# Transposed q and k for the later batch pairs: small block loads and a VectorE transpose in place of TensorE transposes

## The chip, the core and the metric

The kernel runs on one core of a Trainium2 chip. The metric is the device time of one execution in microseconds. The profile is of one execution of the same kernel; its span runs from the first to the last instruction.

## What is computed

The program is a retention block (attention without softmax, with a decay mask) followed by a multiplicative feed-forward block, all in float32; the four weights arrive as float64 and are converted on the chip.

```python
# q, k, v: (8 batches, 8 heads, 576 positions, 64)
scores = (1/8) * q @ k^T ;  D[n,m] = gamma_h ** (n-m) for n >= m, else 0
x = ((scores * D) @ v)            # then (B,H,S,64) -> (4608 tokens, 512)
a = x @ w1 ; b = x @ w2           # 512 -> 1024
out = ((a * b) @ w3) @ w_out      # 1024 -> 1024 -> 512
```

The decay is split into two factors, `decay_q[h, n] = gamma^n / 8` on q and `decay_k[m, h] = gamma^-m` on v, so that only a triangular 0/1 mask is left for the diagonal blocks.

## The kernel before

**Tiling.** The eight batches are taken as four pairs, the 576 positions as five chunks: one short chunk of 64 rows and four of 128. A group `g` is one chunk of one pair, so there are 20 groups; `NC` is 5, and groups 5 to 19 are the "later pairs" that the change touches. For a group, `load` (L106) brings k, q and v, each as a tile of positions by 16 heads by 64, 512 KB for a full chunk. `scale` multiplies q and v by their decays on GpSimd (L171). `front` (L185) transposes k and q on TensorE, sixteen transposes for a group (two tensors, two batches, four head pairs), and ScalarE copies the results out of PSUM into `kT` and `qT` (L188). `state` (L221) adds k^T v to a running state, `score` (L200) multiplies kT by qT, VectorE applies the mask (L203), and `pv` (L249 for the state's part, L256 for the chunk's own part) makes x. `state` is left out for the last chunk of a pair, and the L249 part for the first. The k that `state` reads is the one in natural layout, q is needed only transposed.

**The feed-forward.** `up` (L451) makes a and b for one block of 384 tokens and one block of 256 weight columns, by seven Strassen-like products; VectorE adds them up (L456) and multiplies a by b (L477). `w3_mm` (L406) folds w3 and w_out into one matrix once. `down` (L557) multiplies a*b by that matrix, again in seven products, with VectorE sums around it (L523, L527, L529, L561), and its rows are stored by `store` (L602). `strassen_tokens` (L425) makes sums of x on GpSimd for `up`.

**Order.** The order of instructions on each engine is written out by hand, and every engine takes its own in that order. After the weights' part comes the loop over groups 5 to 19 (L757). An iteration `g` holds: loads of q and k for `g+2`; `scale` of v and `front` for `g+1`; the first half of the iteration's feed-forward items (`work`); `pv(g)`; the load of v for `g+2`; `state(g+1)` and `score(g+1)`; `scale` of q for `g+2`; the second half of the items. The list of items grows as x becomes available: the iterations of groups 5 to 9 have one item each, the later ones two to four.

**Queues and buffers.** Nearly all DMAs are issued from the SP engine's queue, in program order: loads of q, k, v, the weights and the stores of the result. An SP instruction that waits (for a buffer to come free, or for a result to store) holds all that are behind it. The tiles `ld_k`, `ld_q`, `ld_v` have two buffers each; after the first pair, `kT` has one and `qT` two. GpSimd's order around the loop is `scale` of v for `g+1`, `scale` of q for `g+2`, with `strassen_tokens` between them where an item needs it.

Of the kernel before, what the change touches and what calls it, by code (L numbers as in the profile page):

```python
# [8 lines left out]
F32 = mybir.dt.float32  # L9
I32 = mybir.dt.int32  # L10
U32 = mybir.dt.uint32
ALU = mybir.AluOpType
PSUM = bass.MemoryType.PSUM

# [19 lines left out]
def kernel(  # L36
# [13 lines left out]
    nc = tc.nc  # L50
    moe_w1, moe_w2, moe_w3, moe_w_out = (
        w.bitcast(I32).rearrange("r (c t) -> r c t", t=2) for w in (moe_w1, moe_w2, moe_w3, moe_w_out))
    B, H, S, D = q.shape
# [3 lines left out]
    P = 128  # L57
    NP = H // 2
# [3 lines left out]
    NC = (S + P - 1) // P  # L62
    short = S - (NC - 1) * P
    sizes = [short] + [P] * (NC - 1)
    starts = [0] + [short + c * P for c in range(NC - 1)]
    G = NB2 * NC
# [9 lines left out]
    const = ctx.enter_context(tc.tile_pool(name="const", bufs=1))  # L76
# [8 lines left out]
    pools = {}  # L85

    def open_attention(part):
        for nm in ("ld", "fr"):
            pools[nm] = part.enter_context(
                tc.tile_pool(name=nm, bufs=2, side="right", reuse_waits="tile"))  # L90

    open_attention(att_part)
    acc = ctx.enter_context(tc.tile_pool(name="acc", bufs=7, space=PSUM))
    st_ps = ctx.enter_context(tc.tile_pool(name="st_ps", bufs=1, space=PSUM))

    ctx.enter_context(tc.manual_schedule())

    live = {}

    def load(g, names, engine=nc.sync):  # L100
        i, c = divmod(g, NC)
        sz = sizes[c]
        src = {"k": k, "q": q, "v": v}
        for nm in names:
            t = pools["ld"].tile([P, 2 * H, D], F32, tag="ld_" + nm, name="ld_" + nm)
            engine.dma_start(  # L106
                t[:sz], src[nm][2 * i:2 * i + 2, :, starts[c]:starts[c] + sz, :].rearrange("b h p d -> p (b h) d"))
            live[nm, g] = t
# [13 lines left out]
    nc.vector.memset(lim[:, 1:2], 255.0 * 2.0 ** 23)  # L122
    gk = const.tile([P, NC, H], F32, tag="gk", name="gk")
    gq = const.tile([P, NC, H], F32, tag="gq", name="gq")
    dq = ffn.tile([P, 4, 2, TB], F32, tag="c", name="dq", bufs=1).rearrange("p a b s -> p (a b s)")[:H, :S]
    nc.scalar.dma_start(dq, decay_q)
    nc.scalar.dma_start(gk[:short, 0, :], decay_k[:short, :])
# [4 lines left out]
    for c in (0, slice(1, NC)):  # L132
        n = short if c == 0 else P
# [16 lines left out]
    def strassen_weights(fp):  # L150
# [8 lines left out]
        live["S", fp] = True  # L159
        yield  # L160

    def scale(g, nm, scalar=False):
        c = g % NC
        sz = sizes[c]
        t, gam = live[nm, g], {"q": gq, "v": gk}[nm]
        t = t[:sz].rearrange("p (b h) d -> p b h d", b=2)
        if scalar:
            for h in range(H):
                nc.scalar.mul(t[:, :, h, :], t[:, :, h, :], gam[:sz, c, h:h + 1])
            return  # L170
        nc.gpsimd.tensor_tensor(  # L171
            out=t, in0=t, in1=gam[:sz, c].unsqueeze(1).unsqueeze(3).to_broadcast([sz, 2, H, D]), op=ALU.mult)

    def front(g, names="kq"):
        c = g % NC
        sz = sizes[c]
        for nm in names:
            src = live[nm, g]
            dst = pools["fr"].tile([P, 2, NP, P], F32, tag=nm + "T", name=nm + "T",
                                   bufs=1 if nm == "k" and g >= NC else 2)  # L180
            for b in range(2):
                tp = acc.tile([P, NP, P], F32, tag="acc", name="tp")
                for p in range(NP):
                    h = b * H + 2 * p
                    nc.tensor.transpose(tp[:, p, :sz],  # L185
                                        src[:sz, h:h + 2, :].rearrange("p a d -> p (a d)"),
                                        ident[:sz, :sz])
                nc.scalar.copy(dst[:, b, :, :sz], tp[:, :, :sz])  # L188
            live[nm + "T", g] = dst
# [17 lines left out]
    def state(g):  # L207
        c = g % NC
        sz = sizes[c]
        if c == NC - 1:  # L210
            return
        kn, vs = live["k", g], live["v", g]
        if c == 0:
            live["st"] = st_ps.tile([P, 2, NP, D], F32, tag="st", name="st")
        st = live["st"]

        for b in range(2):
            for p in range(NP):
                for j, hs in enumerate(heads):
                    h = b * H + 2 * p + j  # L220
                    nc.tensor.matmul(st[hs, b, p, :], kn[:sz, h, :], vs[:sz, h, :],  # L221
                                     start=(c == 0 and b == 0 and p == 0), stop=(c == NC - 2),
                                     skip_group_check=True)
        sb = pools["fr"].tile([P, 2, NP, D], F32, tag="sb", name="sb")
        nc.scalar.copy(sb, st)
        live["sb", g + 1] = sb

    def pv(g):
        i, c = divmod(g, NC)
        sz = sizes[c]  # L230
        live["x", g] = True
        qT, vs, pm = live["qT", g], live["v", g], live["pm", g]

        parts = []
        for n in range(NB):
            lo, hi = max(starts[c], n * TB), min(starts[c] + sz, (n + 1) * TB)
            if lo < hi:
                m = i * NB + n
                if ("xT", m) not in live:
                    live["xT", m] = xps[m % 4 == 3].tile([P, NP, 2, TB], F32, tag="xT", name="xT")  # L240
                parts.append((live["xT", m], lo - n * TB, lo - starts[c], hi - lo))

        banks = [acc.tile([P, 2, 2, P], F32, tag="acc", name="xps") for r in range(2)]
        order = [(b, n) for b in range(2) for n in range(2)]
        if c > 0:
            for m, (b, n) in enumerate(order):
                for r, j in ((0, 0), (0, 1), (1, 0), (1, 1)):
                    p = 2 * r + n
                    nc.tensor.matmul(banks[r][heads[j ^ r], b, n, :sz], live["sb", g][heads[j], b, p, :],  # L249
                                     qT[heads[j], b, p, :sz], start=(m == 0), stop=False,  # L250
                                     skip_group_check=True)
        for m, (b, n) in enumerate(order):
            for r in range(2):
                for half in range(2):
                    p, j = 2 * r + n, half ^ r
                    nc.tensor.matmul(banks[r][heads[half], b, n, :sz], vs[:sz, b * H + 2 * p + j, :],  # L256
                                     pm[:sz, b, j, p, :sz], start=(c == 0 and m == 0), stop=True,
                                     skip_group_check=True)
        for x, to, fr, n in parts:
            for r in range(2):  # L260
                nc.scalar.copy(  # L261
                    x[:, 2 * r:2 * r + 2, :, to:to + n].rearrange("p n b s -> p b n s"),
                    banks[r][:, :, :, fr:fr + n])
# [272 lines left out]
    def ahead(x, y, n=3):  # L536
        todo_sums = pair_of(x, y)[2]
        for _ in range(min(n, len(todo_sums))):
            aside.append(todo_sums.pop(0))
# [132 lines left out]
    att_part.close()  # L672


    pools["ab3"] = weights_part.enter_context(tc.tile_pool(name="ab3", bufs=1, side="right", reuse_waits="tile"))
    pools["wst"] = w3_part.enter_context(tc.tile_pool(name="wst", bufs=2, side="right", reuse_waits="tile"))
    w3op = ctx.enter_context(tc.tile_pool(name="w3op", bufs=1, reuse_waits="tile"))
# [34 lines left out]
    carry(2, 2)  # L712
    weights_part.close()
    open_attention(ctx)
    for g in (NC, NC + 1):
        load(g, "kqv")
    keep_stores.clear()
    store()
    todo = [(down, (0, 0), (0, 1)), (down, (1, 0), (1, 1)), (down, (0, 2), (1, 2))]
# [18 lines left out]
    def work(n):  # L738
        for _ in range(min(n, len(todo))):
            fn, *args = todo.pop(0)  # L740

            nxt = next((x for x in todo if x[0] is not carry), None)
            if nxt and nxt[0] is down and fn is not carry:
                if fn is down:
                    args.append(nxt[1:])
                else:
                    last = args == [*every[max(nxt[1][0], nxt[2][0])], NQ - 1]
                    ahead(*nxt[1:], 1 if last else 3)
            fn(*args)

    scale(NC, "q")
    scale(NC, "v")
    front(NC)
    state(NC)
    score(NC)
    scale(NC + 1, "q")
    for g in range(NC, G):  # L757
        c = g % NC
        n = -(-len(todo) // (NC - c))
        if g + 2 < G:  # L760
            load(g + 2, "kq")
        if g + 1 < G:
            scale(g + 1, "v")
            front(g + 1)
        work((n + 1) // 2)
        pv(g)
        if g + 2 < G:
            load(g + 2, "v")
        if g + 1 < G:
            state(g + 1)  # L770
            score(g + 1)
        if g + 2 < G:
            scale(g + 2, "q")
        if g == NC + 1:
            strassen_tokens(1, 0)
            todo.extend((up, 1, 0, fp) for fp in range(2))
        work(n // 2)
        if c == NC - 1:
            add_pair(g // NC)
# [44 lines left out]
```

## Time and profile before

The times are those of three runs, the rest is from the page of the profile and from the trace.

| What | Value |
|---|---|
| time, median (lowest to highest) | 888.04 us (887.27 to 888.92) |
| profiled span | 885.9 us |
| transposes of k and of q (L185), 160 each | 21.1 and 20.7 us busy |
| copies of kT and qT out of PSUM on ScalarE (L188), 40 each | 19.9 and 20.3 us busy |
| scaling of q on GpSimd (L171), 18 instructions | 34.8 us busy, 1.93 us each |
| loads of k and q, 512 KB each | 6.5 and 7.1 us from issue to landing |
| packets of all DMAs | 125,555, of which 113,704 under 512 bytes |

Busy times on different engines overlap and can't be added. "Idle before" counts only for an engine that sets the end. Matmul durations overlap one another: sixteen transposes whose mean is 0.27 us follow each other in 1.75 to 1.90 us. The chain that ended last, in order of time, shows how long such a batch holds TensorE.

### The profile page before, as it was taken

What the parts mean: (1) busy time and instruction counts of PE and PEld (TensorE: products, weight loads), DVE (VectorE), ACT (ScalarE), POOL (GpSimd) and SP (SyncE); (2) the same over time, 40 slices, a digit from 0 to 9 for tenths busy, and PEclk for the clock granted to TensorE, in tenths of its full rate; (3) what the DMA queues carried; (4) which work ended last, traced back from release to release, by engine and by line L of the source; (5) the groups of instructions that cost most, each with busy time, mean ns of one, the idle gap of its engine ahead of it and who ended that gap; (6) DMA issues with size and microseconds to landing.
All of it is one profiled execution on the core that took longest, in us unless ns stands there. A gap on an engine that the chain in (4) does not pass through costs nothing.

```text
span 885.9 us, 15255 instructions
## 1 busy us (share of the span) xinstructions
PE 866.6 (98%) x6517; PEld 792.8 (89%) x6517; DVE 433.7 (49%) x763; ACT 212.4 (24%) x426; POOL 111.1 (13%) x82
## 2 busy tenths in 40 slices
PE   5899999999999999999999999999999999999998
PEld 4799999544889999999999999999999999999997
DVE  3799998971543243433434433433433424434343
ACT  3676334552122212111121111211110111001000
POOL 3000020003003223002112121221200101000000
PEclk9999999999999999999999999999999999999999
DMA  9993332427046533134033134022100000000001
GB/s 184 217 229 99 96 118 97 143 95 107 0 108 124 105 60 73 26 72 96 1 72 61 25 72 95 1 57 40 26 24 24 1 24 1 24 24 1 24 1 47
DMA packets 125555, 59.73 MB, mean 67 GB/s; under 512 B 113704, under 2 KB 113704, under 8 KB 125488
## 3 DMA queue, kind: packets, MB, share of 16 engines
q1 hardware_dynamic: 123824, 58.47, 29.9%
q8 instruction: 51, 0.84, 0.4%
q10 hardware_dynamic: 1664, 0.30, 0.2%
q14 instruction: 16, 0.13, 0.1%
HBM read 49.32 MB, written 9.44 MB: 66 GB/s over the span
## 4 chain that ended last, share of the span: by engine, by line
PE 89%; DVE 3%; issue 1%; DMA 1%; ACT 1%; ACTq 0%; SPq 0%; DVEq 0%
PE up L451 45%; PE po L557 24%; PE ps L406 6%; PE xps L256 4%; PE sc L200 3%; PE tp L185 3%; PE xps L249 2%; PE st L221 1%; DVE c L456 1%; PE tp L396 1%; DVE e L341 0%; DMA raw<-in_moe_w_dram 0%; ACT e L330 0%; DVE w L350 0%; DVE ab L477 0%
## 5 line engine op out<-in xcount | busy, mean ns | idle before, releaser
L456 DVE TENSOR_TENSOR c<-up,c 128x384 f32<-128x384 f32 x240 | 133.6, 557 | 224.3 <-PE up L451 218.0
L451 PE MATMUL up<-xT,wA 128*128 128x192 f32 x1152 | 212.6, 328 | 0.9 <-ACT xT L261 0.9
L451 PEld LDWEIGHTS up<-xT,wA 128*128 128x128 f32 x1152 | 191.0, 191 | 3.2 <-ACT xT L261 1.1
L451 PE MATMUL up<-T,wS 128*128 128x192 f32 x768 | 141.7, 328 | 2.1 <-DVE T L425 2.1
L451 PEld LDWEIGHTS up<-T,wS 128*128 128x128 f32 x768 | 128.3, 191 | 2.4 <-issue 2.4
L557 PE MATMUL po<-w3o,ab 128*128 128x256 f32 x456 | 104.1, 380 | 0.3 <-ACT ot L579 0.3
L557 PEld LDWEIGHTS po<-w3o,ab 128*128 128x128 f32 x456 | 85.9, 190 | 12.2 <-ACT ot L579 0.7
L471 ACT COPY c<-up 128x384 f32<-128x384 f32 x48 | 22.9, 477 | 228.1 <-PE up L451 223.9
L561 DVE TENSOR_TENSOR ot<-po,ot 128x256 f32<-128x256 f32 x90 | 38.2, 424 | 74.8 <-PE po L557 74.2
L451 PE MATMUL up<-xT,wS 128*128 128x192 f32 x384 | 70.6, 327 | 0.6 <-DVE c L456 0.5
L451 PE MATMUL up<-T,wA 128*128 128x192 f32 x384 | 70.3, 326 | 0.0
L203 DVE TENSOR_TENSOR pm<-sc,mask 128x512 f32<-128x512 f32 (+1 forms) x80 | 45.5, 629 | 48.0 <-PE sc L200 48.0
L557 PE MATMUL po<-wB,forms 128*128 128x256 f32 x288 | 65.1, 379 | 0.0
L451 PEld LDWEIGHTS up<-xT,wS 128*128 128x128 f32 x384 | 63.6, 190 | 1.5 <-DVE c L456 1.5
L451 PEld LDWEIGHTS up<-T,wA 128*128 128x128 f32 x384 | 63.7, 190 | 0.0
L557 PEld LDWEIGHTS po<-wB,forms 128*128 128x128 f32 x288 | 54.7, 190 | 7.4
L171 POOL TENSOR_TENSOR ld_q<-ld_q,gq 128x1024 f32<-128x1024 f32 (+1 forms) x18 | 34.8, 1931 | 209.7 <-DMA ld_q<-in_q_dram 204.4
L406 PE MATMUL ps<-wo,w3T 128*128 128x512 f32 x128 | 56.4, 593 | 0.2 <-ACT w3T L398 0.2
L171 POOL TENSOR_TENSOR ld_v<-ld_v,gk 128x1024 f32<-128x1024 f32 (+1 forms) x17 | 32.3, 1900 | 176.5 <-DMA ld_v<-in_v_dram 144.1
L425 POOL TENSOR_TENSOR T<-xT,T 128x384 f32<-128x384 f32 x20 | 21.2, 1058 | 228.9 <-PE up L451 227.2
L477 DVE TENSOR_TENSOR ab<-c 128x768 f32<-128x768 f32 x48 | 46.4, 967 | 3.8
L406 PEld LDWEIGHTS ps<-wo,w3T 128*128 128x128 f32 x128 | 23.7, 190 | 27.3 <-issue 26.8
(72 smaller groups left out, 829.1 us busy)
## 6 DMA issues: line engine op xcount, KB each, us to landing
raw<-in_moe_w_dram SPq DMA_DIRECT2D x24, 512.0 KB, 3.8
ld_k<-in_k_dram SPq DMA_DIRECT2D x16, 512.0 KB, 6.5
ld_q<-in_q_dram SPq DMA_DIRECT2D x16, 512.0 KB, 7.1
ld_v<-in_v_dram SPq DMA_DIRECT2D x16, 512.0 KB, 4.7
out_dram<-ot SPq DMA_DIRECT2D x24, 256.0 KB, 2.1
raw<-in_moe_w_dram SPq DMA_DIRECT2D x16, 256.0 KB, 6.4
raw<-in_moe_w_out_dram SPq DMA_DIRECT2D x8, 512.0 KB, 3.5
out_dram<-ot SPq DMA_DIRECT2D x24, 128.0 KB, 2.4
```

Source lines behind the costliest of these rows:

```text
L171: nc.gpsimd.tensor_tensor(out=t, in0=t, in1=gam[:sz, c].unsqueeze(1).unsqueeze(3).to_broadcast([sz, 2, H, D]), op=ALU.mult)
L185: nc.tensor.transpose(tp[:, p, :sz], src[:sz, h:h + 2, :].rearrange("p a d -> p (a d)"), ident[:sz, :sz])
L200: nc.tensor.matmul(sc[j][:sz, p, :sz], kT[hs, b, p, :sz], qT[hs, b, p, :sz], start=True, stop=True)
L203: nc.vector.tensor_mul(pm[:sz, b, j, :, :sz], sc[j][:sz, :, :sz], mask[:sz, :sz].unsqueeze(1).to_broadcast([sz, NP, sz]))
L256: nc.tensor.matmul(banks[r][heads[half], b, n, :sz], vs[:sz, b * H + 2 * p + j, :], pm[:sz, b, j, p, :sz], start=(c == 0 and m == 0), stop ...
L406: nc.tensor.matmul(ps, live["w3T", ft][:, g, :], live["wo"][:, g, :], start=(g == 0), stop=(g == KF - 1))
L451: nc.tensor.matmul(ps[:, w, :], a[:, w, r, :], b[:, r, :], start=(new and w == r == 0), stop=(w == r == 1), skip_group_check=True)
L456: nc.vector.tensor_add(c[:, to], ps, c[:, sb])
L471: nc.scalar.copy(c[:, 0], p1)
L477: nc.vector.tensor_mul(ab[:, 4 * fp:4 * fp + 4, :], c[:, :, 0, :], c[:, :, 1, :])
L557: nc.tensor.matmul(ps[nm], a[A][:, f, :], live["W"][B][:, f, :], start=(f == 0 and not on), stop=(f == NP - 1), skip_group_check=True)
L561: nc.vector.tensor_add(ot[:, to[0], to[1]], ps[nm], ot[:, sb[0], sb[1]])
```

## The change

For groups 5 to 19, q and k are no longer transposed by TensorE. A transpose of 64-wide heads in pairs is a transpose of 128x128 made of a 4 by 4 grid of 32x32 blocks. `load_blocks` lets the DMA put each 32x32 block where it belongs after the transpose, and VectorE transposes within the blocks, one instruction for a whole tensor of a group. Its parts:

- `load_blocks` issues sixteen DMAs for each tensor of a full chunk, eight for a short one. Each fills 32 partitions with eight head pairs by 32 elements, so that a contiguous run is 128 bytes and a DMA holds 32 KB.
- The tiles `bl_k` and `bl_q` have one buffer each, so the loads for the next group wait until VectorE has read the present ones. They are placed right after `front_blocks`.
- `scale_blocks` applies the q decay on GpSimd in the new layout, in two instructions, with factors `gqs` that are loaded once by sixteen small DMAs of single 4-byte elements, at about 100 us.
- `front_blocks` is two VectorE transposes, after the first half of `work` instead of `front` ahead of it.
- k is also still loaded in natural layout for `state`, but not for a pair's last chunk.
- The first pair's groups stay as they were.

```diff
+    gqs = const.tile([P, NP, S // 32], F32, tag="gqs", name="gqs")
...
+    BL = 32
+
+    def load_blocks(g, nm):
+
+        i, c = divmod(g, NC)
+        n = sizes[c] // BL
+        t = pools["ld"].tile([P, 2 * NP, P // BL, BL], F32, tag="bl_" + nm, name="bl_" + nm, bufs=1)
+        src = {"k": k, "q": q}[nm][2 * i:2 * i + 2].rearrange("b (p a) s d -> a (b p) s d", a=2)
+        for a in range(2):
+            for f in range(D // BL):
+                part = (a * (D // BL) + f) * BL
+                for m in range(n):
+                    s0 = starts[c] + m * BL
+                    nc.sync.dma_start(t[part:part + BL, :, m, :],
+                                      src[a, :, s0:s0 + BL, f * BL:(f + 1) * BL].rearrange("m r x -> r m x"))
+        live["bl_" + nm, g] = t
+
+    def scale_blocks(g):
...
+        for b in range(2):
+            part = t[:, b * NP:(b + 1) * NP, :n, :]
+            nc.gpsimd.tensor_tensor(
+                out=part, in0=part, in1=gqs[:, :, n0:n0 + n].unsqueeze(3).to_broadcast([P, NP, n, BL]),
+                op=ALU.mult)
+
+    def front_blocks(g):
...
+        for nm in "kq":
+            dst = pools["fr"].tile([P, 2, NP, P], F32, tag=nm + "T", name=nm + "T", bufs=1 if nm == "k" else 2)
+            nc.vector.transpose(
+                dst[:, :, :, :sizes[c]].rearrange("p b m (n x) -> p (b m) n x", x=BL),
+                live["bl_" + nm, g][:, :, :n, :])
...
+    for a in range(2):
+        for f in range(D // BL):
+            part = (a * (D // BL) + f) * BL
+            for p in range(NP):
+                nc.sync.dma_start(gqs[part:part + BL, p, :], decay_q[2 * p + a].rearrange("(n r) -> r n", r=BL))
...
-    for g in (NC, NC + 1):
-        load(g, "kqv")
+    load(NC, "kv")
+    load_blocks(NC, "k")
+    load_blocks(NC, "q")
+    load(NC + 1, "kv")
...
-    scale(NC, "q")
+    scale_blocks(NC)
     scale(NC, "v")
-    front(NC)
+    front_blocks(NC)
+    load_blocks(NC + 1, "k")
+    load_blocks(NC + 1, "q")
     state(NC)
     score(NC)
-    scale(NC + 1, "q")
+    scale_blocks(NC + 1)
     for g in range(NC, G):
...
-        if g + 2 < G:
-            load(g + 2, "kq")
+        if g + 2 < G and (g + 2) % NC != NC - 1:
+            load(g + 2, "k")
         if g + 1 < G:
             scale(g + 1, "v")
-            front(g + 1)
         work((n + 1) // 2)
+        if g + 1 < G:
+            front_blocks(g + 1)
+        if g + 2 < G:
+            load_blocks(g + 2, "k")
+            load_blocks(g + 2, "q")
         pv(g)
...
         if g + 2 < G:
-            scale(g + 2, "q")
+            scale_blocks(g + 2)
```

More of the change, by code (lines that the diff above doesn't have):

```diff
@@ L160, in strassen_weights @@
         yield
+    BL = 32
[13 more added lines that the diff above has]
+    def scale_blocks(g):
+        c = g % NC
+        n, n0 = sizes[c] // BL, starts[c] // BL
+        t = live["bl_q", g]
+        for b in range(2):
[4 more added lines that the diff above has]
+    def front_blocks(g):
+        c = g % NC
+        n = sizes[c] // BL
+        for nm in "kq":
[3 more added lines that the diff above has]
+                live["bl_" + nm, g][:, :, :n, :])
+            live[nm + "T", g] = dst
     def scale(g, nm, scalar=False):
@@ L179, in front @@
             dst = pools["fr"].tile([P, 2, NP, P], F32, tag=nm + "T", name=nm + "T",
-                                   bufs=1 if nm == "k" and g >= NC else 2)
+                                   bufs=2)
             for b in range(2):
@@ L211, in state @@
             return
-        kn, vs = live["k", g], live["v", g]
+        vs = live["v", g]
+        kn = live["k", g]
         if c == 0:
```

## The prediction

> **What bounds the kernel now.** I read the page's busy times, then the chain of waits that ended last, then its pieces in order of time around the groups that change, then the SP queue's own timeline. The first two:
>
> ```profile
> PE 866.6 (98%) x6517; PEld 792.8 (89%) x6517; DVE 433.7 (49%) x763; ACT 212.4 (24%) x426; POOL 111.1 (13%) x82
> ...
> PE up L451 45%; PE po L557 24%; PE ps L406 6%; PE xps L256 4%; PE sc L200 3%; PE tp L185 3%; PE xps L249 2%; PE st L221 1%; DVE c L456 1%; PE tp L396 1%; DVE e L341 0%; DMA raw<-in_moe_w_dram 0%; ACT e L330 0%; DVE w L350 0%; DVE ab L477 0%
> ```
>
> TensorE is the bound nearly everywhere, and its transposes (tp L185) lie on the chain. The chain in order of time (start, length, what) shows the iterations of groups 5 and 6:
>
> ```profile
> 261.51 1.08 PE xps L256 x32
> 262.59 1.08 PE st L221 x32
> 263.67 1.99 PE sc L200 x32
> 265.65 1.90 PE tp L185 x16
> 267.55 12.09 PE po L557 x56
> 279.64 1.03 PE xps L249 x32
> 280.67 1.90 PE xps L256 x32
> 282.57 0.93 PE st L221 x32
> 283.50 1.99 PE sc L200 x32
> ```
>
> TensorE never pauses, and from one score to the next are 19.8 us. The scores for groups 6 to 11 start at 263.7, 283.5, 303.3, 319.2, 335.5 and 358.7; later ones are 29 us or more apart. So the early iterations leave the least time for a load. Last, the SP timeline (start, length, what), from four short windows:
>
> ```profile
> 243.14 1.18 SPq L602 DMA_DIRECT2D out_dram<-ot  x2
> ...
> 298.24 0.36 SPq L602 DMA_DIRECT2D out_dram<-ot  x1
> ...
> 319.33 0.60 SPq L106 DMA_DIRECT2D ld_v<-in_v_dram  x1
> 319.98 0.85 SPq L106 DMA_DIRECT2D ld_k<-in_k_dram  x1
> ...
> 334.54 0.37 SPq L106 DMA_DIRECT2D ld_v<-in_v_dram  x1
> ```
>
> The stores at 243 and the load at 319.33 cover 64 rows, those at 298 and 334 cover 128. Issuing holds SP for 0.36 us with 128 rows but 0.60 us with 64, although the 64-row ones move half as much. Half the bytes are no cheaper to issue; this decides the forecast.
>
> [...] the load at 319.98 follows the one of 0.60 us at 319.33. [...] A 64-row load lands 4.2 us after its issue here[...]. Before, eight cold 64-row transposes near 9 us took 1.11 us, and sixteen at 244 us took 1.14 us: the factor of two shows.
>
> **What is removed.** The sixteen transposes of each of groups 5 to 19. The chain has them at 1.14, 1.90 four times, 0.98, 1.90, 1.75, 1.75, 1.90, 1.14 and 1.75 four times: 25.2 us, all on the bounding engine. The ScalarE copies of kT and qT (about 0.55 us, four a group) go too, worth nothing by themselves, since ScalarE is 24% busy.
>
> **What is added, off the path.** The factors `gqs`: 16 issues of about 0.6 us, 10 us of SP time among the w_out loads. Those are issued some 5.6 us apart and five buffers deep, so some 22 us ahead of use, and land in 3.5 us: no cost. Packets: 8,192 of 128 bytes a group for the blocks, and q's 2,048 of 256 bytes fall away. The window around the v load at 505 us gives 40.8% of sixteen engines over 6 us for 2,064 packets, 19 ns each. I take 19 ns as the ceiling and half of it as the floor for 128 bytes: 4.9 to 9.7 us a group, under the issue time below. GpSimd: two multiplications for one, the same 1.9 us for a full group.
>
> **What is added on VectorE.** Two transposes a group, an operation this trace does not show. The nearest row is an addition of 128x1024 float32, 1.217 us. [...] I take 1.22[...]. They now sit behind the item's last VectorE work, and score waits for both. After a `down`, VectorE is busy 1.1 us beyond TensorE (last sum 245.08 + 0.42 against 244.38), after an `up` 1.65 us. With 2.5 us for the transposes they are done 3.6 or 4.1 us after the item. `pv` and `state` cover 3.9 us in most iterations, 2.2 at a pair's first chunk, 2.9 where `state` is missing. That leaves waits of 0.3 to 2.0 us: for groups 13 to 19 I add 0.3 + 1.3 + 1.5 + 0.3 + 0.3 + 0.7 = 4.4 us.
>
> **What is added on SP, and the new wait.** Each full group has 32 block DMAs of 32 rows. I price one like the 64-row ones: 0.59 (two in 1.18) to 0.65 us (319.33 to 319.98), middle 0.62, so 19.8 us. The buffers are single, so the loads of the next group start only when the transpose of k has run. Behind the last issue come 2.3 us to landing (a 128 KB store takes 2.4), 1.9 us for q's decay, 1.9 us for v's, which stands behind it on GpSimd, then `state` and score: 2.3 + 1.9 + 1.9 + 0.9 + 0.1 = 7.1 us. Also queued on SP behind the blocks are loads of k and v and stores, 1.6 to 2.6 us an iteration; score on TensorE, and every item behind it, waits for all of this.
>
> Step by step. Group 5 (loads long landed) has score wait 1.6 us for its transposes; it ends at 247.9. Group 6: issue from 246.2, last one 265.4, ready at 272.7 (`state` 1.1). TensorE gets there at 247.9 + 12.1 + 2.2 = 262.2: it waits 10.5. Group 7: SP free at 266.0 + 2.6 = 268.6, last issue 287.8, ready 294.9; TensorE at 274.7 + 12.1 + 3.8 = 290.6: 4.3. Group 8 likewise: ready 317.3 against 312.9: 4.4. Group 9, no `state`: last issue 331.6, ready after 5.5 us at 337.1; TensorE at 331.3: 5.8. Group 10 is short, half the DMAs, ready in time. Group 11: k's buffer is free at 350.8, last issue 370.0, ready 377.3 against 373.6: 3.7. After that the iterations are longer than the 27 us of one round. Waits: 1.6 + 10.5 + 4.3 + 4.4 + 5.8 + 3.7 = 30.3, with the 4.4 above 34.7. [...] Sum: 34.7 + 1.7 - 25.2 = +11.2, so 888.0 becomes 899.
>
> **The rivals.** First, the transposes' time is really gained. If a 32-row DMA is issued like a 128-row one, 0.36 + 0.05 between, a group takes 13.1 us. The same steps then leave waits of 1.6, 4.0, 0, 0.4, 2.4, 2.0 and 4.4, 14.8 in all: 888.0 - 25.2 + 14.8 = 877.6. For it: the kinds of store differ by rows only, and nothing shows 32 rows. Against it: fewer rows went with a longer issue. Second, no change: by the same steps the sums cancel near 0.53 us, a narrow strip. Third, still slower: an issue of 0.8 us[...], 65.7 us of waits, 888.0 - 25.2 + 65.7 + 1.7 = 930; or transposes of several times 1.2 us, which would delay every iteration. The trace's 4.2 us landings and 19 ns packets speak against it, and the many small transfers for it.
>
> **How the numbers follow.** The forecast, an issue of 0.54 to 0.72 us, has 0.49 (890 to 916). The first rival, below 0.52, has 0.33 (875 to 887), no change 0.03, the third 0.15 (over 916). So faster 0.34, same 0.03, slower 0.63. The range 877 to 922 leaves out the best ends of the first rival and most of the third.
>
> **What would show it.** Right: in the SP timeline block DMAs about 0.62 us apart; TensorE idle before score or `state` near 260 to 340 us, over 4 us each, released by GpSimd's v or VectorE's qT, behind a DMA of q; the last 500 us without such waits; tp L185 at 40 instead of 160 for each of k and q. Wrong: a pitch near 0.4 (then 878), StreamTranspose well over 1.3 us, or waits in the later iterations.

## The result, and the profile after

The changed kernel takes 901.59 us (median of four runs, 898.75 to 902.86), the kernel before 888.18 beside it: a ratio of 1.0147, with a 95% interval of 1.0120 to 1.0174. It is slower by some 13 us. The forecast was 899 (877 to 922), with slower as the likeliest outcome. The profiled spans are 885.9 and 900.5 us.

The page of the changed kernel: first the busy times, then a part of the chain that ended last, then the issues of the blocks (source, queue, count, size, median us from issue to landing).

```profile
PE 853.0 (95%) x6277; PEld 777.1 (86%) x6277; DVE 472.9 (53%) x793; ACT 184.2 (20%) x366; POOL 113.5 (13%) x97
PE up L493 40%; PE po L599 22%; SPq L179 7%; PE ps L448 6%; PE sc L241 3%; DMA ld_v<-in_v_dram 2%; PE xps L298 1%; DMA ld_q<-in_q_dram 1%; DVE c L498 1%; DVE kT L198 1%; DMA out_dram<-ot 1%; DVE qT L198 1%; DVE e L383 1%; PE tp L438 1%; PE xps L291 1%
bl_k<-in_k_dram SPq DMA_DIRECT2D x216, 32.0 KB, 2.3
bl_q<-in_q_dram SPq DMA_DIRECT2D x216, 32.0 KB, 2.2
```

TensorE has 240 instructions less and 14 us less busy time, but 47 us of idle time in place of 19. The issue of blocks on SP (L179), which did not exist before, is 7% of the chain. The transposes that were on it are gone.

The SP timeline around groups 6 and 7 (start, length, queue, line, what, how many):

```profile
247.23 8.83 SPq L179 DMA_DIRECT2D bl_k<-in_k_dram  x16
256.16 8.61 SPq L179 DMA_DIRECT2D bl_q<-in_q_dram  x16
264.86 0.40 SPq L109 DMA_DIRECT2D ld_k<-in_k_dram  x1
265.36 2.63 SPq L644 DMA_DIRECT2D out_dram<-ot  x3
268.08 7.99 SPq L179 DMA_DIRECT2D bl_k<-in_k_dram  x16
276.18 7.78 SPq L179 DMA_DIRECT2D bl_q<-in_q_dram  x16
```

SP is hardly idle here (about 0.1 us between these lines). Sixteen blocks take 7.8 to 8.8 us, so one takes 0.49 to 0.56, and a full group 15.9 to 17.5 us. TensorE's timeline, the pieces that waited (the bracket holds the wait in us and what ended it):

```profile
247.94 1.15 PE L241 MATMUL sc<-qT,kT 64*64 64x64 f32 x32 [1.40 <-DVE qT L198]
270.39 1.97 PE L263 MATMUL st<-ld_v,ld_k 128*64 128x64 f32 x32 [7.95 <-POOL ld_v L212]
290.91 1.15 PE L263 MATMUL st<-ld_v,ld_k 128*64 128x64 f32 x32 [0.35 <-POOL ld_v L212]
294.07 3.07 PE L241 MATMUL sc<-qT,kT 64*128 64x128 f32 x32 [2.01 <-DVE qT L198]
319.08 1.98 PE L263 MATMUL st<-ld_v,ld_k 128*64 128x64 f32 x32 [6.13 <-POOL ld_v L212]
336.99 2.06 PE L241 MATMUL sc<-qT,kT 64*128 64x128 f32 x32 [1.16 <-DVE qT L198]
375.14 1.15 PE L263 MATMUL st<-ld_v,ld_k 128*64 128x64 f32 x32 [2.40 <-POOL ld_v L212]
449.75 2.93 PE L493 MATMUL up<-T,wS 128*128 128x192 f32 x8 [3.36 <-POOL T L467]
452.47 2.77 PE L493 MATMUL up<-xT,wA 128*128 128x192 f32 x8
```

These are 24.8 us of waiting, and six shorter waits after 460 us add 2.8: 27.6 in all. The second number of each line shows a second cost. Behind a long wait the same work is slower: `state` takes 1.97 us instead of 1.15, and the first two batches of the `up` at 449.75 take 2.93 and 2.77 us, where such a batch takes 1.46 in the kernel before. Added up over the batches behind these waits this is about 7.9 us (1.9, 1.7 and 1.5 in groups 6 to 8, 2.8 at 450 us). The granted clock agrees: 0.68 between 261 and 270 us, 0.56 up to 275, 0.50 between 449 and 455, and 1.00 over the stretch from 455 to 900.

How long the way from the last block to score is, the chain that ended last shows for group 6 (start, length, what):

```profile
263.50 2.80 DMA bl_q<-in_q_dram
266.42 2.06 POOL bl_q L189 x2
268.48 1.87 POOL ld_v L212
270.39 1.97 PE st L263 x32
272.37 2.98 PE sc L241 x32
```

In which groups did it go? The starts of score, before and after, are 263.6 and 272.3 for group 6; 303.3 and 321.0 for group 8; 358.7 and 376.2 for group 11; 676.6 and 690.7 for group 19. So 17.6 us are lost by group 11, and only 3 are won back behind it, although 13.5 us of transposes are gone there too.

### The profile page after: what moved, and what is told of

The parts are those of the page before. It is cut to its first block, busy times and chain, and to the rows that moved or that the text cites. A ratio compares the mean times of both kernels' runs of the same rounds, so it can differ in the third digit from the quotient of the medians.

```text
span 900.5 us, 15339 instructions
## 1 busy us (share of the span) xinstructions
PE 853.0 (95%) x6277; PEld 777.1 (86%) x6277; DVE 472.9 (53%) x793; ACT 184.2 (20%) x366; POOL 113.5 (13%) x97
## 2 busy tenths in 40 slices
DMA packets 218455, 65.32 MB, mean 73 GB/s; under 512 B 206600, under 2 KB 206600, under 8 KB 218384
## 4 chain that ended last, share of the span: by engine, by line
PE 75%; DVE 7%; SPq 7%; DMA 5%; issue 3%; POOL 2%; ACT 1%; DVEq 0%; POOLq 0%; ACTq 0%
PE up L493 40%; PE po L599 22%; SPq L179 7%; PE ps L448 6%; PE sc L241 3%; DMA ld_v<-in_v_dram 2%; PE xps L298 1%; DMA ld_q<-in_q_dram 1%; DVE c L498 1%; DVE kT L198 1%; DMA out_dram<-ot 1%; DVE qT L198 1%; DVE e L383 1%; PE tp L438 1%; PE xps L291 1%
## 5 line engine op out<-in xcount | busy, mean ns | idle before, releaser
L493 PE MATMUL up<-xT,wA 128*128 128x192 f32 x1152 | 214.9, 330 | 1.1 <-ACT xT L303 1.0
L493 PEld LDWEIGHTS up<-xT,wA 128*128 128x128 f32 x1152 | 193.0, 192 | 4.3 <-ACT xT L303 1.3
L189 POOL TENSOR_TENSOR bl_q<-bl_q,gqs 128x512 f32<-128x512 f32 (+1 forms) x30 | 29.5, 1004 | 438.2 <-DMA bl_q<-in_q_dram 367.7
L513 ACT COPY c<-up 128x384 f32<-128x384 f32 x48 | 22.9, 478 | 231.1 <-PE up L493 226.9
L519 DVE TENSOR_TENSOR ab<-c 128x768 f32<-128x768 f32 x48 | 49.5, 1030 | 3.8
L506 ACT COPY c<-up 128x384 f32<-128x384 f32 x48 | 22.9, 477 | 133.1 <-PE up L493 84.9
L241 PE MATMUL sc<-qT,kT 64*128 64x128 f32 (+1 forms) x640 | 42.7, 289 | 7.1 <-DVE qT L198 7.0
L241 PEld LDWEIGHTS sc<-qT,kT 64*128 64x128 f32 (+1 forms) x640 | 39.0, 199 | 9.7 <-issue 4.4
```

The costliest lines, as they stand in the source:

```text
L189: nc.gpsimd.tensor_tensor(out=part, in0=part, in1=gqs[:, :, n0:n0 + n].unsqueeze(3).to_broadcast([P, NP, n, BL]), op=ALU.mult)
L241: nc.tensor.matmul(sc[j][:sz, p, :sz], kT[hs, b, p, :sz], qT[hs, b, p, :sz], start=True, stop=True)
L493: nc.tensor.matmul(ps[:, w, :], a[:, w, r, :], b[:, r, :], start=(new and w == r == 0), stop=(w == r == 1), skip_group_check=True)
L506: nc.scalar.copy(c[:, 0], p1)
L513: nc.scalar.copy(c[:, 0], p1)
L519: nc.vector.tensor_mul(ab[:, 4 * fp:4 * fp + 4, :], c[:, :, 0, :], c[:, :, 1, :])
```

## The experiments

All times are medians; each ratio is to the kernel before, measured beside it (887.1 to 887.7 us).

**k's blocks in twice as many DMAs.** The data and its 128-byte packets stay.

```diff
-                    nc.sync.dma_start(t[part:part + BL, :, m, :], ...)
+                    for h0 in range(0, 2 * NP, NP if nm == "k" else 2 * NP):
+                        hs = slice(h0, h0 + (NP if nm == "k" else 2 * NP))
+                        nc.sync.dma_start(t[part:part + BL, hs, m, :], ...)
```

> The block DMAs of k are cut in two along the head pairs: 48 DMAs a full group instead of 32, the same bytes, the same packets of 128 bytes. My theory: 16 more issues at 0.4 to 0.5 us make a round 6 to 8 us longer, which TensorE waits for in each of groups 6 to 9 and 11 and partly in later ones: 925 to 945 us. Rival (packets are the limit): 900 to 903, since they are the same.

Measured: 962.9 us, ratio 1.0850 (1.0832 to 1.0868). SP's timeline for group 6:

```profile
245.57 15.62 SPq L181 DMA_DIRECT2D bl_k<-in_k_dram  x32
261.29 8.95 SPq L181 DMA_DIRECT2D bl_q<-in_q_dram  x16
```

And two of the waits in TensorE's timeline:

```profile
276.20 1.98 PE L265 MATMUL st<-ld_v,ld_k 128*64 128x64 f32 x32 [13.84 <-POOL ld_v L214]
492.93 2.93 PE L495 MATMUL up<-T,wS 128*128 128x192 f32 x8 [10.00 <-POOL T L469]
```

A block of half the size costs the same 0.49 us to issue. The data did not change (all packets of the run went from 218,455 to 221,912, 1.6% more) and the time rose by 61 us, so the rival is out: what counts is the number of issues. It rose by more than I expected because the later waits grew too, as the second wait shows: GpSimd's sums `T` for `up` stand behind v's decay, v's load behind the blocks.

**q's blocks from ScalarE's queue.**

```diff
-                    nc.sync.dma_start(t[part:part + BL, :, m, :],
+                    (nc.scalar if nm == "q" else nc.sync).dma_start(t[part:part + BL, :, m, :],
```

> The sixteen block DMAs of q are issued from ScalarE's queue instead of SP's, at the same place in the order; bytes, packets, buffers and VectorE work are unchanged. My theory: SP's serial issue (about 0.53 us for each of 32) sets when a group is ready. With half of it on another queue a round falls from about 17 to about 9 us, the waits before state and score of groups 6 to 9 (16.8 + 4.6 us) and most of the cold clock after them go: 880 to 890 us. First rival (the transfer of 8,192 packets of 128 bytes is the limit, whichever queue issues it): about 901. Second rival (VectorE's transposes and their place cost it): about 900.

Measured: 957.7 us, ratio 1.0793 (1.0757 to 1.0828). No theory named that. One line of ScalarE's timeline:

```profile
240.59 19.13 ACTq L179 DMA_DIRECT2D bl_q<-in_q_dram  x23
```

And TensorE's waits after 400 us (engine, line, what it waited for: us in total, times, longest):

```profile
PE po L599 <- ACT ot L621: 19.4, 4, 6.8
PE up L493 <- ACT c L506: 11.0, 4, 3.9
```

ScalarE's queue was held by the blocks for 19 us at a stretch, and the copies out of PSUM that TensorE's next products need stood behind them. Over the whole loop TensorE waited 32.6 us for the copy into `ot` and 17.1 for that into `c`. A round then held SP for 9.8 us instead of 15.9 to 17.5, and yet nothing was gained, because ScalarE has work of its own behind its queue. The expectation looked at the DMAs alone and left this out. Since two things changed, this run says nothing for or against serial issue.

**q's decay behind v's on GpSimd**, without and with v's load on another queue.

```diff
         if g + 1 < G:
+            scale_blocks(g + 1)
             front_blocks(g + 1)
...
-        if g + 2 < G:
-            scale_blocks(g + 2)
```

> On GpSimd the decay of q for the next group moves behind the decay of v and behind the sums of x that up needs; nothing else is changed. My theory says that GpSimd's order is a second part of the loss: the up at 450 us (waits 3.4 us, then 2.8 us at half clock), state of group 8 behind the four sums (about 4 us), and v's decay behind q's (1.9 us a group): 889 to 895 us. If only the issue on SP counts, the wait just moves from state to score: 899 to 902.

Measured: 914.9 us, ratio 1.0304 (1.0280 to 1.0329), slower than the changed kernel. The expectation failed: in the changed kernel q's decay uses the time in which v, issued behind the blocks, is still landing. In the new place it starts after v's decay and, in group 11, also after four sums, and score waits 28.9 us for qT in six places before 400 us.

```diff
-            load(g + 2, "v")
+            load(g + 2, "v", nc.scalar)
```

> Moving q's decay behind v's alone made the kernel 13 us slower than the changed one; my reading is that v's load is issued behind 32 block DMAs and lands some 5 us after the blocks. Here v's load is issued from ScalarE's queue after pv, so it no longer stands behind the blocks, and q's decay stands last as in that run. By this reading v, state and the sums of x are all ready before the blocks, and score waits for the blocks alone: 887 to 895 us. Rival (q's decay in its late place is itself what cost the 13 us): 910 or more.

Measured: 900.0 us, ratio 1.0140 (1.0123 to 1.0158), not to be told from the changed kernel. The wait at 450 us for `T` is gone, and `state` waits for v nowhere, as I had expected; the gain is not there. First TensorE's waits with their total before 400 us, then two of SP's over 240 to 400:

```profile
PE sc L241 <- DVE qT L198: 26.8, 6, 10.9
SPq L179 <- DVE kT L198: 13.4, 3, 5.6
SPq L179 <- DMA ld_v<-in_v_dram: 11.6, 4, 5.4
```

Everything but the blocks is on time now, and score waits for the blocks alone, with q's decay and transpose right behind them: 26.8 us, against 21.4 for `state` and score together in the changed kernel. So v and GpSimd's sums are not the only thing that is late: with them out of the way TensorE waits for the blocks instead. The last line is odd: nothing in a block of k or q depends on v, and yet blocks wait for its loads, 11.6 us in all. I come back to it. Since this run has that wait of its own, what v's place in the queue costs by itself stays open.

**The old path in groups 5 to 9**, the blocks from group 10 on.

```diff
+        if g < OLD:            # OLD = 10, in scale_blocks
+            scale(g, "q")
+            return
...
+            if g + 1 < OLD:
+                front(g + 1)
```

> Groups 5 to 9 keep TensorE's transposes and the load of q in natural layout, groups 10 to 19 have the blocks. My theory: the short iterations of groups 5 to 9 cost more than they save (about 17 us lost by group 9 against 8.5 us saved there), and from group 10 on the saving of 16.7 us is partly eaten by waits of about 9 us: 880 to 887, faster than the kernel before. Rival (the blocks cost the same in every group): half-way between the two kernels or above, 894 to 897.

Measured: 892.3 us, ratio 1.0060 (1.0041 to 1.0079). 8.7 us of the 13.4 come back (each against the kernel before that was measured beside it), although the single buffer that q has in this kernel costs a new wait of 5.1 us in group 6. So the short iterations hold most of the loss. But it isn't faster than before: from the score of group 10 to the end it gains 2.5 us on the kernel before, not the 15.4 of the transposes of groups 11 to 19. The waits that it shares with the changed kernel are there (3.9 us for `T`, 2.5 for `qT`).

**Earlier issue: transposes in place, blocks two groups ahead.** The place of kT and qT becomes further buffers for the blocks.

```diff
-        t = pools["ld"].tile([...], tag="bl_" + nm, bufs=1)
+        t = pools["ld"].tile([...], tag="bl_" + nm, bufs=2 if nm == "k" else 3)
...
+            t = live["bl_" + nm, g]
+            nc.vector.transpose(t[:, :, :n, :], t[:, :, :n, :])
...
+        if g + 2 < G:          # ahead of the item of iteration g
+            load_blocks(g + 2, "k")
+            load_blocks(g + 2, "q")
```

> VectorE transposes within the loaded tile instead of into kT and qT; the room of these makes two buffers for k's blocks and three for q's, so that the blocks for g+2 are issued at the start of iteration g, ahead of the feed-forward item, and groups 5 and 6 ahead of the loop. The number of DMAs, packets and VectorE instructions is unchanged. My theory (the loss is a serial issue that may only begin when single buffers come free): the waits before groups 6 to 9 (21.4 us) and after 440 us (3.7) go, those for VectorE's transposes (about 5 us) stay: 872 to 882 us. Rivals (the number of DMAs or packets as such, or VectorE's transposes, cost the time wherever they stand): 897 or more.

> As the kernel with transposes in place, and on GpSimd the decay of q for a group stands behind v's decay and the sums of x, next to its use. The blocks have landed long before here, so the order on GpSimd should only help where the decay of q for g+2 waits for its DMAs ahead of other work: 0 to 6 us below the kernel in place alone, 868 to 880. If GpSimd's order no longer matters: within 1 us of it.

Measured: 916.7 us (ratio 1.0328, 1.0313 to 1.0343) and 917.7 (1.0339, 1.0324 to 1.0355). They don't test the theory, since the larger pool lies where an earlier stage still works: the loads of group 5, issued at 205 us in the changed kernel, wait until 243.67. GpSimd's order makes no difference here. With every buffer where the changed kernel has it:

> The kernel with transposes in place again, but each buffer where the changed kernel has it (one of k's and one of q's in the place of bl_k and bl_q, the others in the place of kT and qT). In the first such kernel the loads of group 5 had to wait until 243 us for memory of an earlier stage, 40 us later than in the changed kernel, and 80 blocks were issued at once behind it; here group 5 is loaded before 220 us, and only the blocks of group 6 wait until about 243. SP issues the same 32 blocks a group, but no longer waits for VectorE between them: a round of some 20 us against the 18 to 20 us of TensorE's iterations, so waits of 2 to 4 us in groups 6 to 9 and none for blocks later: 876 to 888 us. Rival (the number of issues costs the same wherever they stand): 898 or more.

Measured: 895.9 us, ratio 1.0088 (1.0065 to 1.0112). It is 6 us better than the changed kernel, but no more. SP's timeline around 298 us:

```profile
288.75 9.33 SPq L187 DMA_DIRECT2D bl_q<-in_q_dram  x16
298.18 1.74 SPq L650 DMA_DIRECT2D out_dram<-ot  x3
```

And TensorE's waits before 400 us:

```profile
PE po L605 <- ACT ot L627: 13.8, 3, 6.6
PE sc L247 <- issue: 4.3, 3, 1.9
PE sc L247 <- DVE qT L206: 1.3, 1, 1.3
```

The view puts three waits of score under "issue", but each ends with a transpose. In group 11 score begins at 372.96 after a wait of 1.9 us, and VectorE's timeline there is:

```profile
369.62 0.96 DVE L525 TENSOR_TENSOR ab<-c 128x768 f32<-128x768 f32 x1
370.50 1.24 DVE L206 STREAM_TRANSPOSE bl_k<-bl_k 128x1024 f32<-128x1024 f32 x1
371.66 1.20 DVE L206 STREAM_TRANSPOSE bl_q<-bl_q 128x1024 f32<-128x1024 f32 x1
```

So 5.6 us of waits for transposes are left, here not because the blocks are late but because VectorE comes to them only behind its own last work. Instead of the waits for blocks, the next `down` waits for `ot`, which has one buffer and cannot be written until it is stored, and the stores stand on SP behind the blocks (the one at 298.18 directly behind sixteen of them). So I moved the stores:

```diff
-            nc.sync.dma_start(*stores.pop(0))
+            nc.scalar.dma_start(*stores.pop(0))
```

> The second kernel with transposes in place and blocks two groups ahead (895.9 us), with the stores of the result issued from ScalarE's queue instead of SP's. In it TensorE waited 13.8 us, in three down products, for ScalarE's copy into ot, which waited for stores that stood on SP behind sixteen or more block DMAs. My theory: with the stores off that queue these waits and some 4 us of half clock behind them go, and up to 4 us of waits for blocks take their place: 874 to 884 us. Rival (32 block DMAs a group cost TensorE the same time whatever stands behind them): 892 or more, the waits moving to score.

Measured: 911.5 us, ratio 1.0273 (1.0244 to 1.0302): worse. The waits for `ot` went, as expected, but others came. TensorE's waits and SP's, before 400 us:

```profile
PE st L269 <- POOL ld_v L218: 28.2, 3, 10.8
SPq L187 <- DMA out_dram<-ot: 43.8, 8, 19.9
```

Block DMAs on SP wait for stores on ScalarE's queue, 43.8 us in eight places, 19.9 us in one. As with v above, no data joins the two. What does is in the built program. These are four of its instructions, the sixth and the tenth block of k for group 6 and the first and the third of three stores, with the semaphores that each waits for:

```
SP  L187 DMACopy kT<-in_k_dram 32x8x32 [waits DMAHW6_49]
SP  L187 DMACopy kT<-in_k_dram 32x8x32 [waits DMAHW2_49]
ACT L650 DMACopy out_dram<-ot 64x512 [waits DMAHW6_49,DVE_49]
ACT L650 DMACopy out_dram<-ot 128x512 [waits DMAHW2_49,DVE_49,Activation_49]
```

In this program the 589 DMAs of both queues (537 on SP's, 52 on ScalarE's) share eight completion semaphores (DMAHW0 to 7), and 546 of them are issued only after a wait on their own one, that is, for the earlier DMA that used it. The trace fits: five blocks of k for group 6 are issued from 223.06 us on, the sixth only at 245.23, after the first of three stores that ScalarE issued from 242.94 on. So in this kernel moving a store to another queue doesn't free the blocks behind it. This is read from the program and the waits; no run gave the queues semaphores of their own.

**q alone by blocks.** k is in SBUF in natural layout anyway, for `state`, and is transposed by TensorE as before. q's blocks have two buffers and are issued at the start of an iteration.

```diff
         if g + 2 < G:
             load(g + 2, "k")
+            load_blocks(g + 2, "q")
         if g + 1 < G:
             scale(g + 1, "v")
+            front(g + 1, "k")
...
-        for nm in "kq":        # in front_blocks
+        for nm in "q":
```

> Only q comes by blocks; k, which is loaded in natural layout for state anyway, is transposed by TensorE as before. Sixteen block DMAs a group instead of 32; their tile has two buffers and is loaded at the start of an iteration. Half the transposes, 12.6 us, leave TensorE. My theory: at half the issues SP is no bound (8.5 us a round), only waits for VectorE's last transpose of up to 5 us and a little cold clock remain: 877 to 884 us. Rival (blocks in any number cost more than they save): 889 or more.

Measured: 879.6 us, ratio 0.9911 (0.9896 to 0.9926): faster than both kernels, as the theory said. Its busy times on the page:

```profile
PE 854.4 (97%) x6397; PEld 778.8 (89%) x6397; DVE 452.6 (52%) x778; ACT 199.6 (23%) x396; POOL 112.8 (13%) x97
```

All waits of TensorE between 230 and 400 us:

```profile
PE sc L241 <- DVE qT L198: 1.9, 3, 0.9
PE up L493 <- DVE c L498: 0.7, 1, 0.7
PE po L599 <- DVE ab L565: 0.5, 1, 0.5
```

With one more of 0.2 us later, TensorE waits 3.3 us from 230 us on instead of 27.6, and its clock is full (1.00, the mean of the profiled execution). Issuing a round takes SP 8.8 to 10.8 us. Of the 12.6 us of q's transposes, 8.3 us of span arrive.

**k by blocks too where iterations are long**, in two ways. The first takes q and k in place with blocks two groups ahead, k by blocks from group 10 on.

> q by blocks in groups 5 to 19, k by blocks only in groups 10 to 19, where iterations are longer than a round; k of groups 5 to 9 by TensorE; transposes in place, blocks issued two groups ahead. 12.6 us of q's transposes and 8.4 of k's leave TensorE. My theory: SP is a bound nowhere (16 blocks a group, 8.5 us, in the short iterations), only waits of up to 5 us for VectorE's last transpose remain: 870 to 878 us, below the kernel with q alone. Rival (32 blocks a group also cost in the long iterations, as the waits after 440 us in the changed kernel): 880 or more.

Measured: 888.0 us, ratio 0.9998 (0.9985 to 1.0011), the same as before. The second q buffer lies where memory is freed late, so that group 6's blocks were issued only at 244.6 us with stores behind them: one wait of 6.2 us for `ot`. As for k in the long iterations, a second run starts from the kernel with q alone:

```diff
+        if g >= OLD:           # OLD = 10, in front_blocks
+            t = live["bl_k", g]
+            nc.vector.transpose(t[:, :, :n, :], t[:, :, :n, :])
...
+        if OLD <= g + 2 < G:   # behind score(g + 1)
+            load_blocks(g + 2, "k")
```

> The kernel with q alone by blocks (879.6 us), and in groups 10 to 19 also k by blocks: loaded into kT itself right behind the last score that reads it, transposed in place by VectorE one iteration later. 8.2 us of k's transposes leave TensorE. My theory: what made the changed kernel slow is that in groups 6 to 9 a round of 32 issues is longer than TensorE's iteration; from group 10 on iterations are 16 to 50 us and 32 issues fit, so only waits for VectorE's last transpose (1.2 us in five groups) are added: 872 to 877 us. Rival (blocks of k cost as much as they save also in long iterations, since what stands behind them is late): 878 to 884.

Measured: 879.8 us, ratio 0.9913 (0.9897 to 0.9928): the rival's forecast. The 8.2 us of k's transposes bring nothing. TensorE's timeline at group 13's score, first of this kernel, then of the kernel with q alone:

```profile
441.64 2.46 PE L250 MATMUL sc<-qT,kT 64*128 64x128 f32 x32 [0.18 <-PE st L272]
```

```profile
440.54 2.06 PE L241 MATMUL sc<-qT,kT 64*128 64x128 f32 x32
```

Score takes 0.3 to 0.5 us longer in most of these groups. Since k's tile was filled by sixteen DMAs and transposed where it lies, the program lets each of the first two matmuls wait for all eight DMA semaphores besides the others, though they were met long ago. The trace has these as wait instructions of their own, nine for group 13's score, each for one or two semaphores and most of them 51 ns long (the view of L250 from 440 to 443 us). Four of the nine stand between the first matmul and the second. In the changed kernel and with q alone the same matmuls wait for one or two semaphores (twelve such instructions at L241 in the changed kernel's whole run, 51 ns each).

The waits grow too. In group 11 score waits 1.9 us where q alone cost 0.8, and runs in part at half clock (3.72 us; granted clock 0.67 from 357 to 361 us); in group 14 it waits 1.1 us where q alone cost nothing. Both are again under "issue", and both end with the transpose of q (357.26 us in group 11, score at 357.36), which now stands behind that of k on VectorE. With 1.1 us of shorter waits the ten groups lose about 9 us where they save 8.2. This is read from the trace; no run took the extra semaphore waits or the second transpose away by itself.

## Why the prediction came out right

The sign and the mechanism were right. That the total came within 3 us is in part luck, since misses cancel: the waits of groups 5 to 11 were forecast 8.9 us too long, the late waits 1.8 and the cold clock 6.2 us too short, and 4.3 us of the measured difference stand in no term.

**The bound and what is removed: right.** `tp` L226 is down to 40 for each of k and q, all before 69 us.

**The pitch of 0.62 us: too high.** It is 0.49 to 0.56. The range given for the forecast began at 0.54, and at 0.53 my own steps cancel to no change. So the price of an issue alone would have led to no change; the sign held because what follows the last block takes longer, and slow work after a wait costs more, than I had put. 64-row DMAs were not the right row: 32-row ones are quicker to issue than those and slower than the 128-row ones (0.40 here). That half the bytes are no cheaper held: 16 KB blocks cost the same.

**7.1 us from the last issue to score: too low.** In group 6 it took 8.8 us, as landing took 2.8 us and `state` ran at half clock (1.97 us, granted clock 0.50), in group 8 more than 12. I had named v's load behind the blocks on SP, but put no time on it, and not seen the four sums on GpSimd: they run from 313.19 to 317.16, v's decay for group 8 only then, and `state` at 319.08. In group 7 score waited for VectorE: sums of 0.68 to 0.69 us before take 1.35, 1.43 and 2.27 us between 286 and 291, while GpSimd works on q and v (2.51 and 2.00 us) beside it. Why they are longer was not shown: they overlap GpSimd's work in time, and no run separates the two. The chain that ended last puts a store that landed at 291.28 in this place, but VectorE was busy without a pause up to then, and in the kernel before the same last sum ran at 299.5 while a store issued at 298.24 (3.5 us to landing) was under way.

**Waits, group by group.** Predicted 1.6, 10.5, 4.3, 4.4, 5.8, 0 and 3.7 for groups 5 to 11, measured 1.4, 8.0, 2.4, 6.1, 1.2, 0 and 2.4: 30.3 against 21.4. The late ones, 4.4 for groups 13 to 19: the waits for VectorE came to 2.5, smaller than forecast, but 3.7 us for `T` were missing from my list, so 6.2. "The last 500 us without such waits" was wrong, and waits in the later iterations were one of my signs of being wrong. Of the waits of "over 4 us each" between 260 and 340 us there were two, not four. That later iterations are 29 us or more apart was misread: the scores of groups 13 and 14 start 28.0 us apart.

**The cold clock, 1.7 us once: far too low.** It is about 7.9 us. The 1.7 us in the sum, for slow work on TensorE behind a wait, was the author's estimate; no trace was named for it. It was counted once, on the thought that while SP is the bound slow work only shortens the next wait. This failed because SP is not the bound from wait to wait: its blocks start when VectorE has read k, VectorE follows TensorE's item, and so slow work delays the next round too: between 230 and 400 us SP's block issues waited 15.1 us, in four places, for VectorE's transpose of k. Behind each of the three waits of over 3 us (7.95, 6.13 and 3.36) the granted clock is 0.50. Shorter waits did it too: 0.35 and 2.01 us in group 7 (score 3.07 us, clock 0.64 from 294.0 to 297.1); behind the 2.40 us in group 11 the clock stayed at 1.00 (`state` 1.15 us).

**The sum.** Predicted 34.7 + 1.7 - 25.2 = +11.2. Measured 21.4 + 6.2 + 7.9 - 25.2 = +10.3 of the +14.6 us in the spans. One us lies ahead of 245 us (the store at 243.14 comes at 244.22); it is there before 70 us, ahead of what the change touches. The other 3.3 I can't assign to a term, but they go mostly with the waits: where nothing is waited for (groups 10, 12 and 19) the time from score to score changed by that of the transposes to 0.01 us (group 15 is 0.2 us off), and in the groups with a wait mostly 0.1 to 0.4 us come on top of wait and slow work.

**Costed at nothing.** VectorE's transposes take 1.24 and 1.20 us (estimate 1.22). The factors `gqs` hold SP for 10.4 us and nobody waits for them. The packets are not what costs, as the doubled issues show. That ScalarE's copies are worth nothing fits: from 240 us on TensorE waited for none of them in the kernel before.

**The rivals.** A pitch of 0.41 (877.6) was out from the first block on, 0.8 (930) too. The chances are 0.01 off: 0.49 and 0.15 make 0.64 for slower, not 0.63, and the 0.33 for faster stands as 0.34. A way that I didn't see is to take half of the change: 879.6.

## What to carry to other kernels

By these runs, price a load that is cut into small pieces by its number of issues on its queue (here about 0.49 us each, at 32 KB as at 16 KB), and compare a whole round, with everything that queues behind it (the next tensor, the stores, what a helper engine does in order), with the shortest iteration, not the mean. Half of such a change can be worth more than all of it: here q by blocks gains 1%, and k by blocks on top costs it, or brings nothing where iterations are long. Moving issues to another engine's queue did not pay here where that engine had work that others wait for (q's blocks on ScalarE's queue, 957.7 us against 901.6), nor where the DMAs of the two queues wait for each other's semaphores (the stores, 911.5 against 895.9).

## What was not expected of the hardware

- Issue time of a DMA by its form: about 0.49 us a block of 32 rows at 32 KB (changed kernel) as at 16 KB (k's blocks in twice as many DMAs), 0.60 for 64 rows (kernel before), 0.40 for 128 rows of 512 KB (changed kernel).
- With k by blocks in the late groups, a wait instruction on semaphores that are long met took 51 ns on TensorE; with nine of them ahead of its first two matmuls a score of 2.06 us took 2.46.
- With both queues issuing blocks at once, one took 0.61 us on SP (sixteen in 9.8) and 0.58 on ScalarE's queue (sixteen in 9.34), so the two together issued one every 0.30 us, not every 0.25. These times hold waits: between 230 and 400 us SP's block issues waited 16.3 us, in 39 places, for blocks under way, as the shared semaphores would have it. An estimate: eight semaphores, each taken for the 2.4 us to landing, allow one block every 0.30 us.
- Half clock behind a single wait of 1.9 us, with k by blocks in the late groups (score 3.72 us); behind 2.1 us in another kernel score stayed at 2.06 us. In the clock record of the changed kernel TensorE is at half clock from 264.2 to 274.4 us, 294.9 to 298.3, 315.4 to 322.2 and 448.5 to 455.3: 10.2, 3.4, 6.8 and 6.8 us, all multiples of 3.4, as are the times between them. So in this record the clock changes on a grid of 3.4 us and not with the wait itself. How long a wait has to be for it stays open.
- VectorE's transpose of 32x32 blocks of float32 took 1.24 us for 128x1024 in the changed kernel, about as long as an addition of that size in the kernel before (1.22).
